# Spreading the sums of w_out over four pairs of blocks of chunk 1, and taking the last product and store in two pieces over two queues

## Chip, cores and metric

One core of one Trainium2 chip runs the whole program. The metric is device time in microseconds (us) of one execution. Lower is better. Runs of one kernel here spread over 0.3 to 5.6 us from one execution to the next, so differences below that are read from stages inside the profiles, as explained below.

## The reference

Everything is float32.

```python
# q, k, v: (8 batches, 8 heads, 576, 64)
kv = einsum('bhsd,bhse->bhde', k, v)
o = einsum('bhsd,bhde->bhse', q, kv)
rms = sqrt(mean(o * o, axis=-1) + 1e-6)
x = (o / rms * g_norm)                     # -> (4608, 512)
gate = 1 / (1 + exp(-(x @ w_gate)))        # w_gate, w_val: (512, 1536)
out = (gate * (x @ w_val)) @ w_out         # w_out: (1536, 512)
```

## The kernel before

The 4608 rows are worked in chunks of 512 (`G`). Chunk 0 is computed plainly. From chunk 1 on both layers use a seven-product scheme for 2x2 blocked matrices, so seven block products do the work of eight, at the price of sums of the operands. The sums of `x` and of the hidden activations are made for each chunk. The sums of `w_out` (`t2w`) are made once, in chunk 1, since chunk 0 still reads the plain `w_out`.

The first layer of a chunk runs six pairs of blocks. A pair issues p1, p6, p2, p7, p5, p4, p3, each for two blocks. After each of these seven comes one `slot()`, in which one small step of other work is put into the engines' streams: a step of the attention for the next chunk, or, in chunk 1, a sum of `w_out`. VectorE (DVE) reads the products out of PSUM, the memory that TensorE writes, and TensorE (PE) can begin a later product only when the bank that it writes has been read.

```python
def slot():
    if fill:
        fill.popleft()()

# first layer, one pair
one, two = block(f), block(f + NF2)
for i, (p, r) in enumerate(zip(one[0], two[0])):
    p()
    r()
    slot()
    # ... at i == 4 and 5: GpSimd makes the sums of w_gate, w_val for the next pair
one[1]()          # h * gate, VectorE, 128x512, both inputs in SBUF
two[1]()
h_sums(c, f)      # four sums on VectorE, 128x256

# the second layer, end of one group of rows
product(pc, lambda f: s12[c, f][:, t1], t2w[1], True)
tt(out=o2[:, d2], in0=pc, in1=o2[:, d2], op=ALU.add)
product(pb, lambda f: gv[c, f + NF2][:, t2], t2w[4], False)
tt(out=o2[:, d1], in0=pb, in1=o2[:, d1], op=ALU.add)
store(c, 2 + g, o2)
product(pc, lambda f: s4[c, f][:, t1], b[2, 2], False)
tt(out=o1[:, d2], in0=pc, in1=o1[:, d2], op=ALU.add)
store(c, g, o1)   # 256 KB, all issued on SyncE's queue

# the eight half sums of w_out, ahead of the attention steps in the same queue
def t2w_sum(i, in0, in1):
    for fs in (slice(0, NF2 // 2), slice(NF2 // 2, NF2)):
        fill.append(lambda fs=fs: tt(out=t2w[i][:, fs], in0=in0[:, fs], in1=in1[:, fs], op=ALU.subtract))
t2w_sum(3, b22, b12)
t2w_sum(1, b12, b11)      # written over b12
t2w_sum(2, b22, t2w[1])
t2w_sum(4, b21, t2w[2])
for c in range(1, NG):
    if c + 1 < B:
        feed(c + 1, at_ps)        # appends the steps of attention
    first_layer_fast(c)
    sums_of(c + 1)
    second_layer_fast(c)
    flush()
```

Of the kernel before, what the change touches and what calls it, by code (L numbers as in the profile page):

```python
# [14 lines left out]
ALU = mybir.AluOpType  # L15
# [4 lines left out]
def kernel(  # L20
# [11 lines left out]
    nc = tc.nc  # L32

    B, H, S, HD = q.shape
    T, DM = out.shape
# [3 lines left out]
    NJ = 6  # L39
# [13 lines left out]
    NG = T // G  # L53
# [237 lines left out]
    fill = deque()  # L291
# [5 lines that stand above are left out]
    def feed(b, at_ps):  # L297

        for n in range(NHP * b, NHP * b + NHP, 2):
            both = []  # L300

            def tile_of(i, both=both):
                def ps(kind):
                    if kind != "kv":
                        return at_ps(kind)
                    if not both:
                        both.append(at_ps(kind))
                    return both[0][:, :, HD * i:HD * i + HD]
                return ps

            one, two_ = (attention(n + i, tile_of(i)) for i in range(2))

            def kv_of_both(one=one, two_=two_):
                one[0]()
                two_[0]()

            fill.extend([kv_of_both, one[1], two_[1]])
            for steps in (one, two_):

                fill.extend(steps[2:-2] + [lambda: None] * 2 + steps[-2:])  # L320
# [7 lines left out]
    def gv_tile(c, f):  # L328
        gv[c, f] = hp.tile([P, G], FP32, tag="gv", name="gv")
        return gv[c, f]  # L330

    def sg_tile():
        return sb.tile([P, G], FP32, tag="sg", name="sg", bufs=4)

    def store(c, t, ot):

        r0 = 0
        while r0 < P:
            b, s = divmod(G * c + P * t + r0, S)
            j, p = divmod(s, NP)  # L340
            n = min(P - r0, NP - p)
            dst = out[S * b:S * b + S, :].rearrange("(p j) d -> j p d", j=NJ)[j, p:p + n, :]
            nc.sync.dma_start(out=dst, in_=ot[r0:r0 + n])
            r0 += n


    psum_at = ctx.enter_context(tc.tile_pool(name="psum_at", bufs=1, space=bass.MemoryType.PSUM))
# [3 lines left out]
    def at_ps(kind):  # L351
        return psum_at.tile([P, 2, 512], FP32, tag="at", name="at")
# [15 lines left out]
    def mm_ps():  # L368
        return psum.tile([P, 512], FP32, tag="mm", name="mm", bufs=6)
# [21 lines left out]
    def plain(c, f, ps):  # L391

        blk = Plain(c, f, ps)
        for at in range(2 * NMT):
            blk.mm(*divmod(at, NMT))
            if at in (0, 2) and late:
# [8 lines left out]
    steps = {"KV": KV, "KVO": KV_OUT, "Q": Q, "QO": Q_OUT, "U": U, "SQ": U_SQUARE, "SUM": U_SUM, "ROOT": U_ROOT,  # L405
             "NORM": U_NORM, "X": X, "XO": X_OUT}
# [16 lines left out]
    for token in order.split():  # L423
        name = token.rstrip("0123456789.")
        n = [int(i) for i in token[len(name):].split(".")]
        f = n[0]
        if name == "b":
            if f not in blks:
# [4 lines left out]
                else:  # L433
                    t = at_ps(None) if f else two0
# [57 lines left out]
    DH = DM // 2  # L492
    h1, h2 = slice(0, GH), slice(GH, G)
    tt = nc.vector.tensor_tensor
    sx, tw, s12, s4 = {}, {}, {}, {}

    def quarters(c):
        return {(i, j): xT[c][:, NK * (j - 1):NK * j, GH * (i - 1):GH * i] for i in (1, 2) for j in (1, 2)}
# [18 lines left out]
    def first_layer_fast(c):  # L517
        s, a = sx[c], quarters(c)

        def block(f):  # L520

            d = {}
            pa, pb, pc = (mm_ps()[:, h1] for _ in range(3))
            bg, bv = w["wg", f], w["wv", f]

            def product(ps, wt, xs, new):
                for m in range(NK):
                    nc.tensor.matmul(ps, wt[:, m, :], xs[:, m, :], start=(new and m == 0), stop=(m == NK - 1),  # L528
                                     skip_group_check=True)


            def p1():
                product(pa, bg[:, 0:NK], a[1, 1], True)
                d["sg"] = sg_tile()
                nc.scalar.copy(out=d["sg"][:, h2], in_=pa)  # L535

            def p6():
                product(pb, tw[f, 2], s[:, 1], True)
                d["h"] = gv_tile(c, f)
                tt(out=d["h"][:, h1], in0=pb, in1=d["sg"][:, h2], op=ALU.add)  # L540

            def p2():
                product(pa, bg[:, NK:], a[1, 2], False)
                nc.scalar.activation(out=d["sg"][:, h1], in_=pa, func=AF.Sigmoid)  # L544

            def p7():
                product(pb, tw[f, 3], a[2, 1], False)
                tt(out=d["h"][:, h2], in0=pb, in1=d["sg"][:, h2], op=ALU.add)  # L548

            def p5():  # L550
                product(pc, tw[f, 1], s[:, 0], True)
                tt(out=d["h"][:, h2], in0=pc, in1=d["h"][:, h2], op=ALU.add)

            def p4():
                product(pb, tw[f, 4], a[2, 2], False)
                tt(out=d["sg"][:, h2], in0=pb, in1=d["sg"][:, h2], op=ALU.add)  # L556
                nc.scalar.activation(out=d["sg"][:, h2], in_=d["sg"][:, h2], func=AF.Sigmoid)  # L557

            def p3():
                product(pc, bv[:, NK:], s[:, 2], False)  # L560
                tt(out=d["h"][:, h1], in0=pc, in1=d["h"][:, h1], op=ALU.add)  # L561

            def end():
                tt(out=d["h"], in0=d["h"], in1=d["sg"], op=ALU.mult)  # L564

            return [p1, p6, p2, p7, p5, p4, p3], end

        for f in range(NF2):
# [6 lines that stand above are left out]
                if f + 1 < NF2 or c + 1 < NG:  # L575
                    n = (f + 1) % NF2
                    if i == 4:
                        for k_ in (1, 2, 3):
                            w_sum(n, k_)
                            w_sum(n + NF2, k_)  # L580
                    elif i == 5:
                        w_sum(n, 4)
                        w_sum(n + NF2, 4)
            one[1]()
            two[1]()
            h_sums(c, f)
# [12 lines left out]
    def second_layer_fast(c):  # L599
        b = {(j, n): w2[:, NF2 * (j - 1):NF2 * j, DH * (n - 1):DH * n] for j in (1, 2) for n in (1, 2)}  # L600
        d1, d2 = slice(0, DH), slice(DH, DM)
        for g in range(2):
            t1, t2 = slice(P * g, P * g + P), slice(GH + P * g, GH + P * g + P)
            pa, pb, pc = (mm_ps()[:, 0:DH] for _ in range(3))

            def product(ps, hs, ws, new):
                for f in range(NF2):
                    nc.tensor.matmul(ps, hs(f), ws[:, f, :], start=(new and f == 0), stop=(f == NF2 - 1),  # L608
                                     skip_group_check=True)
                    if f % 3 == 2:  # L610
                        slot()

            product(pa, lambda f: gv[c, f][:, t1], b[1, 1], True)
            o2 = sg_tile()
            nc.scalar.copy(out=o2[:, d1], in_=pa)
            product(pb, lambda f: s12[c, f][:, t2], t2w[2], True)
            o1 = sg_tile()
            tt(out=o1[:, d2], in0=pb, in1=o2[:, d1], op=ALU.add)
            product(pa, lambda f: gv[c, f + NF2][:, t1], b[2, 1], False)
            nc.scalar.copy(out=o1[:, d1], in_=pa)  # L620
            product(pb, lambda f: gv[c, f][:, t2], t2w[3], False)
            tt(out=o2[:, d2], in0=pb, in1=o2[:, d1], op=ALU.add)
            product(pc, lambda f: s12[c, f][:, t1], t2w[1], True)
            tt(out=o2[:, d2], in0=pc, in1=o2[:, d2], op=ALU.add)
            product(pb, lambda f: gv[c, f + NF2][:, t2], t2w[4], False)
            tt(out=o2[:, d1], in0=pb, in1=o2[:, d1], op=ALU.add)
            store(c, 2 + g, o2)
            product(pc, lambda f: s4[c, f][:, t1], b[2, 2], False)
            tt(out=o1[:, d2], in0=pc, in1=o1[:, d2], op=ALU.add)
            store(c, g, o1)  # L630

    def sums_of(c):
        if c < NG:
            fill.append(lambda: fill.extendleft(reversed(x_sums(c))))
# [6 lines left out]
    for t in range(G // P):  # L641
# [3 lines left out]
        ot = sg_tile()  # L645
# [5 lines left out]
    t2w = {i: sums.tile([P, NF2, DH], FP32, name=f"t2w{i}", bufs=1) for i in (2, 3, 4)}  # L651
    t2w[1] = b12

    def t2w_sum(i, in0, in1):
        for fs in (slice(0, NF2 // 2), slice(NF2 // 2, NF2)):
            fill.append(lambda fs=fs: tt(out=t2w[i][:, fs], in0=in0[:, fs], in1=in1[:, fs], op=ALU.subtract))  # L656

    t2w_sum(3, b22, b12)
    t2w_sum(1, b12, b11)
# [4 lines left out]
    for c in range(1, NG):  # L664
        if c + 1 < B:
            feed(c + 1, at_ps)
        first_layer_fast(c)
        sums_of(c + 1)
        second_layer_fast(c)
        flush()  # L670
# [30 lines left out]
```

## Time and profile before

The median is 1112.08 us in the three runs first given, and 1112.33 us over six runs (1112.03 to 1114.88) with those made beside the changed kernel.

To compare kernels closely I cut each profile's span at two marks that the chain of waits shows: the first product of chunk 1, and the first product of chunk 2. That gives three stages.

| stage of the kernel before | us | what lies in it |
|---|---|---|
| front, to chunk 1's first product | 161.02 | loads, first attention, chunk 0 |
| chunk 1 | 123.55 | the sums of w_out, wherever they are put |
| rest, from chunk 2's first product to the end of the span | 825.49 | chunks 2 to 8, the last store |

The mark that ends chunk 1 is this line of the kernel before's chain of waits (start in us, length in us, what ran):

```profile
284.57 1.73 PE mm L528 x8
```

(The rest is taken from the view by windows, which gives a stretch to 0.01 us; the page prints the span to 0.1 only.) The other views of the kernel before are in the prediction.

### The profile page before, as it was taken

Reading aid. Unit: us, or ns where it says so; the run is one execution under the profiler, and the core shown is the slowest. Engines: PE = TensorE matmul, PEld = TensorE weight load, DVE = VectorE, ACT = ScalarE, POOL = GpSimd, SP = SyncE. Lnnn points to the kernel's source line nnn. Section 1 sums busy time; section 2 is a strip of 40 time slices with the busy share of each in tenths; the row PEclk is TensorE's granted clock in tenths of the full one; section 3 lists DMA queues with packets and bytes.
Section 4 is the critical chain, followed back from the end, with each engine's and each line's share of the span. In section 5 each row is a group of like instructions: output and inputs, shape, how many; then the busy total and the mean of one; then the engine's idle time right before and its main releaser. Section 6 shows DMA issues by size and latency. Waiting matters only on the chain.

```text
span 1110.1 us, 15195 instructions
## 1 busy us (share of the span) xinstructions
PE 1099.9 (99%) x5806; PEld 914.9 (82%) x5806; DVE 571.4 (51%) x1157; ACT 319.2 (29%) x615; POOL 279.3 (25%) x390
## 2 busy tenths in 40 slices
PE   8999999999999999999999999999999999999998
PEld 7644458888888888888888888888888888888887
DVE  4887758652355415552456336541555256615541
ACT  4754421421243213340333124321333021101110
POOL 0000025440244204330344024420444044404410
PEclk9999999999999999999999999999999999999999
DMA  9954312021201020201211020202000000010001
GB/s 248 270 173 155 146 39 54 12 54 31 73 12 54 21 73 21 54 12 29 64 46 30 19 73 12 54 16 77 22 11 1 26 13 1 1 31 8 1 1 39
DMA packets 71596, 57.61 MB, mean 52 GB/s; under 512 B 40804, under 2 KB 65380, under 8 KB 71524
## 3 DMA queue, kind: packets, MB, share of 16 engines
q1 hardware_dynamic: 71360, 56.64, 19.1%
q8 instruction: 47, 0.77, 0.3%
q14 instruction: 29, 0.21, 0.1%
q10 hardware_dynamic: 160, 0.00, 0.0%
HBM read 47.19 MB, written 9.44 MB: 51 GB/s over the span
## 4 chain that ended last, share of the span: by engine, by line
PE 96%; DVE 2%; issue 1%; DMA 0%; ACT 0%; SPq 0%; DVEq 0%; ACTq 0%
PE mm L528 51%; PE mm L608 26%; PE mm L379 6%; PE mm L471 4%; PE at L250 2%; PE at L379 2%; PE at L221 2%; PE at L235 1%; PE at L276 1%; PE two L250 1%; DMA q<-in_q_dram 0%; DVE gv L564 0%; PE two L221 0%; PE two L235 0%; DVE t2w L656 0%
## 5 line engine op out<-in xcount | busy, mean ns | idle before, releaser
L514 POOL TENSOR_TENSOR tw<-gv 128x256 f32<-128x256 f32 x192 | 140.0, 740 | 779.9 <-PE mm L528 628.1
L528 PE MATMUL mm<-xT,tw 128*128 128x256 f32 x768 | 182.4, 380 | 1.0 <-DVE gv L540 1.0
L528 PE MATMUL mm<-sx,tw 128*128 128x256 f32 x768 | 182.4, 380 | 0.0
L528 PE MATMUL mm<-xT,gv 128*128 128x256 f32 x768 | 181.6, 379 | 0.0
L528 PEld LDWEIGHTS mm<-xT,gv 128*128 128x128 f32 x768 | 145.5, 190 | 20.1 <-issue 0.5
L528 PEld LDWEIGHTS mm<-xT,tw 128*128 128x128 f32 x768 | 143.3, 190 | 20.3 <-issue 1.8
L528 PEld LDWEIGHTS mm<-sx,tw 128*128 128x128 f32 x768 | 144.1, 190 | 19.0
L514 POOL TENSOR_TENSOR tw<-gv,tw 128x256 f32<-128x256 f32 x192 | 144.4, 773 | 0.0
L557 ACT ACTIVATE sg<-sg 128x256 f32<-128x256 f32 x96 | 39.9, 417 | 213.1 <-DVE sg L556 213.1
L548 DVE TENSOR_TENSOR gv<-mm,sg 128x256 f32<-128x256 f32 x96 | 40.8, 425 | 99.8 <-PE mm L528 99.8
L528 PE MATMUL mm<-sx,gv 128*128 128x256 f32 x384 | 90.9, 379 | 0.0
L608 PE MATMUL mm<-t2w,gv 128*128 128x256 f32 x384 | 89.0, 379 | 0.0
L608 PE MATMUL mm<-w,gv 128*128 128x256 f32 x384 | 88.3, 379 | 0.0
L608 PE MATMUL mm<-w,s 128*128 128x256 f32 x384 | 88.1, 379 | 0.0
L608 PEld LDWEIGHTS mm<-w,s 128*128 128x128 f32 x384 | 72.9, 190 | 9.9
L608 PEld LDWEIGHTS mm<-t2w,gv 128*128 128x128 f32 x384 | 72.5, 190 | 9.6
L608 PEld LDWEIGHTS mm<-w,gv 128*128 128x128 f32 x384 | 72.4, 190 | 9.6
L535 ACT COPY sg<-mm 128x256 f32<-128x256 f32 x96 | 35.8, 373 | 154.4 <-PE mm L528 154.4
L528 PEld LDWEIGHTS mm<-sx,gv 128*128 128x128 f32 x384 | 72.1, 190 | 9.4
L564 DVE TENSOR_TENSOR gv<-gv,sg 128x512 f32<-128x512 f32 x96 | 78.7, 860 | 0.2
L561 DVE TENSOR_TENSOR gv<-mm,gv 128x256 f32<-128x256 f32 x96 | 40.7, 424 | 47.9 <-PE mm L528 47.5
L544 ACT ACTIVATE sg<-mm 128x256 f32<-128x256 f32 x96 | 36.3, 384 | 100.5 <-PE mm L528 100.5
(96 smaller groups left out, 1137.0 us busy)
## 6 DMA issues: line engine op xcount, KB each, us to landing
k<-in_k_dram SPq DMA_DIRECT2D x32, 288.0 KB, 4.6
v<-in_v_dram SPq DMA_DIRECT2D x32, 288.0 KB, 4.8
q<-in_q_dram SPq DMA_DIRECT2D x64, 144.0 KB, 3.1
st<-in_moe_w_gate_dram SPq DMA_DIRECT2D x12, 512.0 KB, 5.4
st<-in_moe_w_val_dram SPq DMA_DIRECT2D x12, 512.0 KB, 6.9
st<-in_moe_w_out_dram SPq DMA_DIRECT2D x12, 512.0 KB, 4.1
out_dram<-sg SPq DMA_DIRECT2D x24, 192.0 KB, 2.3
out_dram<-sg SPq DMA_DIRECT2D x24, 128.0 KB, 2.4
```

What stands on the lines that cost most here:

```text
L250: nc.tensor.matmul(d["u"][:, i], qT[:, M * i:M * i + MU], kvs[n % 2], start=True, stop=True)
L379: nc.tensor.matmul(self.ps[i], w[("wg", "wv")[i], self.f][:, m, :], xT[self.c][:, m, :], start=(m == 0), stop=(m == NMT - 1), skip_group_c ...
L471: nc.tensor.matmul(ps[t], gv[0, f][:, P * t:P * t + P], w["wo", f], start=(f == 0), stop=(f == NFT - 1), skip_group_check=True)
L514: nc.gpsimd.tensor_tensor(out=tw[f, i], in0=b[in0], in1=b[in1] if isinstance(in1, tuple) else tw[f, in1], op=ALU.subtract)
L528: nc.tensor.matmul(ps, wt[:, m, :], xs[:, m, :], start=(new and m == 0), stop=(m == NK - 1), skip_group_check=True)
L535: nc.scalar.copy(out=d["sg"][:, h2], in_=pa)
L544: nc.scalar.activation(out=d["sg"][:, h1], in_=pa, func=AF.Sigmoid)
L548: tt(out=d["h"][:, h2], in0=pb, in1=d["sg"][:, h2], op=ALU.add)
L557: nc.scalar.activation(out=d["sg"][:, h2], in_=d["sg"][:, h2], func=AF.Sigmoid)
L561: tt(out=d["h"][:, h1], in0=pc, in1=d["h"][:, h1], op=ALU.add)
L564: tt(out=d["h"], in0=d["h"], in1=d["sg"], op=ALU.mult)
L608: nc.tensor.matmul(ps, hs(f), ws[:, f, :], start=(new and f == 0), stop=(f == NF2 - 1), skip_group_check=True)
```

## The change

The intent is, first, that VectorE should never have a row of sums of w_out ahead of the adds that free PE's banks: the eight sums are put into slots 3 and 4 of each of the first four pairs, two per pair. Second, that the program should end sooner after the last arithmetic: the left half of the last rows is stored as soon as it is done, the last two products on the right half are cut into two halves of 128 columns, and the stores of the last pieces alternate over two queues.

```diff
-    def store(c, t, ot):
+    def store(c, t, ot, cols=slice(0, DM), queues=(nc.sync,)):
 ...
-            nc.sync.dma_start(out=dst, in_=ot[r0:r0 + n])
+            queues[i % len(queues)].dma_start(out=dst, in_=ot[r0:r0 + n, cols])
 ...
+            last = (c, g) == (NG - 1, 1)
+            parts = [slice(0, DH // 2), slice(DH // 2, DH)] if last else [slice(0, DH)]
+            pcs = [mm_ps()[:, 0:x.stop - x.start] for x in parts]
 ...
+            if last:
+                store(c, g, o1, d1)
 ...
-            product(pc, lambda f: s12[c, f][:, t1], t2w[1], True)
-            tt(out=o2[:, d2], in0=pc, in1=o2[:, d2], op=ALU.add)
+            for pc, x in zip(pcs, parts):
+                product(pc, lambda f: s12[c, f][:, t1], t2w[1][:, :, x], True)
+                o2x = o2[:, DH + x.start:DH + x.stop]
+                tt(out=o2x, in0=pc, in1=o2x, op=ALU.add)
 ...
-            product(pc, lambda f: s4[c, f][:, t1], b[2, 2], False)
-            tt(out=o1[:, d2], in0=pc, in1=o1[:, d2], op=ALU.add)
-            store(c, g, o1)
+            for pc, x in zip(pcs, parts):
+                product(pc, lambda f: s4[c, f][:, t1], b[2, 2][:, :, x], False)
+                y = slice(DH + x.start, DH + x.stop)
+                tt(out=o1[:, y], in0=pc, in1=o1[:, y], op=ALU.add)
+                if last:
+                    store(c, g, o1, y, (nc.sync, nc.scalar))
+            if not last:
+                store(c, g, o1)
 ...
+    w2_sums = deque()
 ...
-            fill.append(lambda fs=fs: tt(out=t2w[i][:, fs], ...))
+            w2_sums.append(lambda fs=fs: tt(out=t2w[i][:, fs], ...))
 ...
+        if c == 1:
+            steps = list(fill)
+            fill.clear()
+            while w2_sums or steps:
+                fill.append(w2_sums.popleft() if w2_sums and len(fill) % 7 in (3, 4) else steps.pop(0))
         first_layer_fast(c)
```

The change adds one line above the first layer's code, so line 528 of the kernel before is line 529 after, and so on (540 is 541, 564 is 565); the second layer's product, 608, is 613.

More of the change, by code (lines that the diff above doesn't have):

```diff
@@ L333, in sg_tile @@
         return sb.tile([P, G], FP32, tag="sg", name="sg", bufs=4)
-    def store(c, t, ot):
-        r0 = 0
+    def store(c, t, ot, cols=slice(0, DM), queues=(nc.sync,)):
+        r0 = i = 0
         while r0 < P:
@@ L341, in store @@
             n = min(P - r0, NP - p)
-            dst = out[S * b:S * b + S, :].rearrange("(p j) d -> j p d", j=NJ)[j, p:p + n, :]
-            nc.sync.dma_start(out=dst, in_=ot[r0:r0 + n])
+            dst = out[S * b:S * b + S, :].rearrange("(p j) d -> j p d", j=NJ)[j, p:p + n, cols]
+            queues[i % len(queues)].dma_start(out=dst, in_=ot[r0:r0 + n, cols])
             r0 += n
+            i += 1
     psum_at = ctx.enter_context(tc.tile_pool(name="psum_at", bufs=1, space=bass.MemoryType.PSUM))
@@ L603, in second_layer_fast @@
             t1, t2 = slice(P * g, P * g + P), slice(GH + P * g, GH + P * g + P)
-            pa, pb, pc = (mm_ps()[:, 0:DH] for _ in range(3))
+            pa, pb = (mm_ps()[:, 0:DH] for _ in range(2))
+            last = (c, g) == (NG - 1, 1)
+            parts = [slice(0, DH // 2), slice(DH // 2, DH)] if last else [slice(0, DH)]
+            pcs = [mm_ps()[:, 0:x.stop - x.start] for x in parts]
             def product(ps, hs, ws, new):
@@ L652 @@
     t2w[1] = b12
+    w2_sums = deque()
     def t2w_sum(i, in0, in1):
         for fs in (slice(0, NF2 // 2), slice(NF2 // 2, NF2)):
-            fill.append(lambda fs=fs: tt(out=t2w[i][:, fs], in0=in0[:, fs], in1=in1[:, fs], op=ALU.subtract))
+            w2_sums.append(lambda fs=fs: tt(out=t2w[i][:, fs], in0=in0[:, fs], in1=in1[:, fs], op=ALU.subtract))
     t2w_sum(3, b22, b12)
```

## The prediction

> **What bounds the kernel now.** I read the page first: engine shares, then the chain that ended last.
>
> ```profile
> PE 1099.9 (99%) x5806; PEld 914.9 (82%) x5806; DVE 571.4 (51%) x1157; ACT 319.2 (29%) x615; POOL 279.3 (25%) x390
> PE 96%; DVE 2%; issue 1%; DMA 0%; ACT 0%; SPq 0%; DVEq 0%; ACTq 0%
> ```
>
> TensorE (PE) is 99% busy and 96% of the chain, at full clock. Nothing here removes a matmul, so only PE's own waits and the end of the program can change. Next, the waits of PE in 161 to 246 us, the first layer of chunk 1 (the stretch the first half of the change touches); the same view for 284 to 366 us, chunk 2, lists none.
>
> ```profile
> PE mm L528 <- DVE gv L540: 1.0, 2, 0.7
> PE at L235 <- DVE kv L227: 0.8, 1, 0.8
> ```
>
> The chain for the same stretch shows where:
>
> ```profile
> 161.02 8.65 PE mm L528 x40
> ...
> 175.44 2.36 DVE gv L564 x2
> ...
> 179.38 0.87 DVE t2w L656
> 180.25 0.35 DVE gv L540
> 180.60 0.14 issue
> 180.74 3.69 PE mm L528 x16
> ...
> 220.79 0.43 DVE gv L540
> ```
>
> At 180.74 PE waits for VectorE (DVE), which is late because eight sums of w_out (L656) stand ahead of its other work; by then the last of them is in the way. At 220.8 it waits for the same kind of add (L540), after a head's normalization, with no w_out sum near. At 235 it waits for the two copies of a head's kv. The timeline says what a sum of w_out costs: 0.95 us alone, 1.31 to 1.50 us where GpSimd (POOL) runs beside it, as here:
>
> ```profile
> 165.79 0.95 DVE L656 TENSOR_TENSOR w<-w 128x768 f32<-128x768 f32 x1
> ...
> 171.93 1.50 DVE L656 TENSOR_TENSOR t2w<-w 128x768 f32<-128x768 f32 x1
> 172.58 2.13 POOL L514 TENSOR_TENSOR tw<-gv 128x256 f32<-128x256 f32 x2
> ```
>
> Last, the end, in the timeline:
>
> ```profile
> 1103.45 2.75 PE L608 MATMUL mm<-w,s 128*128 128x256 f32 x12
> 1103.65 0.42 DVE L626 TENSOR_TENSOR sg<-mm,sg 128x256 f32<-128x256 f32 x1 [2.17 <-PE mm L608]
> 1104.10 3.41 SPq L343 DMA_DIRECT2D out_dram<-sg  x4
> 1106.24 0.42 DVE L629 TENSOR_TENSOR sg<-mm,sg 128x256 f32<-128x256 f32 x1 [2.17 <-PE mm L608]
> ```
>
> The last add ends at 1106.66, the last of four store issues on one queue at 1107.51, the span at 1110.1: 3.4 us after the last arithmetic.
>
> **What the Trainium skill says.** "TensorE: Matmul & The Clock Gate", section LDWEIGHTS: a weight load costs its columns over 1.2, 107 ns for 128. The trace agrees when spacing is read instead of duration: ten warm-up loads of 128x128 take 1.20 us, that is (1.20 - 0.19) / 9 = 0.112 us apart, though each is drawn 0.19 long. "SBUF — State Buffer", section Who interferes with whom: a VectorE instruction with two SBUF inputs contends with a GpSimd instruction that reads SBUF; the 0.95 against 1.31 to 1.50 us agrees. "DMA: Bandwidth & Descriptors", section Issuing engines are not separate DMA queues: issuing on several engines saves only the issue time. No run yet shows a store on the second queue. Same page, Anatomy of one DMA: about 2.0 us of a transfer is fixed; the stores here land in 1.6 to 3.7 us, median 2.3, the last two about 2.2 and 2.0.
>
> **The change, part 1: the sums of w_out.** Before, seven sums fill the slots of the first pair of blocks and one the second's; the first of them is free, as it runs at 150.75, before chunk 1 starts. After, the order on VectorE is: no sum ahead of chunk 1; two in each of the first four pairs, after the two adds of p7 and after the two adds of p5. The steps of attention start eight slots earlier and meet the old order again at slot 26. PE's work is the same, only its order differs. So I wrote out the order of each engine for both kernels and added durations: a product of one block 4 x 0.216 = 0.86 us (seven products of two blocks 12.1), adds from PSUM 0.42, L564 0.66 alone and 1.04 beside GpSimd, the four sums of h 0.36 apart, reduce 0.81, reciprocal 0.23, normalization 0.83, sums of w_out 0.95 first and 1.49 second (the second falls where GpSimd has begun), table load 1.28, root 0.30, sigmoid 0.43, x copies 1.05, and 0.2 from PE's end to a reader. For the kernel before this gives waits of 0.69 at 179.9, 0.57 at 220.7, 0.99 at 233.9, with small ones 2.81 in all, and the second layer at 245.11 (trace: 245.32). So the sheet is good to some 0.2 us here. For the changed kernel it says:
> - First pair: VectorE ends its sums of h at 179.3, and the add that frees the bank at 179.8, while PE, with the kv and u matmuls now inside, asks for it at 181.5. The 0.69 is gone.
> - Second pair: second sum of w_out until 187.1, both adds of p4 until 188.0, sigmoid 188.4, table load and root 190.1, reciprocal and normalization 191.3, two L564 192.6, sums of h 194.0, add of the next p6 194.45. PE wants the bank at 194.07: a new wait of 0.48 with latency.
> - Third pair: second sum until 200.2, adds of p4 201.0, sigmoid 201.5, the x copies behind it on ScalarE (ACT) until 202.5. The transposes of q, in the slot after, need the bank that these copies read; PE is there at 201.46: a new wait of 1.26. The order of the changed kernel lists that wait on ScalarE.
> - Fourth pair: two sums now precede the normalization: the wait of 0.57 grows to 0.80. The one of 0.99 stays.
>
> Sum 3.93 against 2.81: 1.1 us slower. With 1.30 for the contended sum it is 246.03 against 245.11, 0.9 slower; with 0.95, even. I take +0.8.
>
> **Part 2: the last product and store.** The last group's s12 and s4 products each become two halves of 128 columns: 24 matmuls at the weight load's 0.112 = 2.69 us in place of 12 x 0.216 = 2.59, +0.1 each, +0.2 on the path. The last add covers 128 columns: 256 cost 0.425 and 1 ns per further column (0.69 for 512), so 0.29: -0.13. The store of the left half goes out some 10 us earlier, the first quarter 1.3 us earlier; what is left is 64 KB in place of 256 KB, on two queues. The second issue (1107.1 to 1107.5) no longer stands behind the first: -0.4. The data of the last store move from 1107.55 to 1108.6; a quarter of them, in rows of 512 bytes, perhaps 0.4 in place of 1.0, partly the same saving as the issue: -0.4 more. Sum -0.75. No WAR wait appears in the order: the last adds wait for PE alone.
>
> Total: 1112.08 + 0.8 - 0.75 = 1112.1 us.
>
> **The rivals.**
> - The spread does what it intends: the wait at 180.74 goes and none comes. For it: half of VectorE's time is free on average, and chunk 2 runs with no wait. Against it: VectorE's slack in a pair with a head's work (12.1 + 1.1 of PE against some 9.5) is about as long as two sums. It would give -1.0 here and, with the tail, 1110.3.
> - Weight loads bind the halves: if each really took its drawn 0.19 us, 48 x 0.19 = 9.1 us in place of 5.2, +3.9 and 1115.5. Against it: the spacing of 0.112, and ten matmuls of L250 with 128 columns and new weights in 1.09 us.
> - The second queue is slow to start: its only transfers before (g_col, at the program's start) took 0.58 us to issue and 3.6 us to land, in tiny pieces. If the last piece lands so, the tail loses its gain and up to 1 us more: 1113.5. Against it: those were 4-byte rows at a busy start.
>
> **Range and chances.** Part 1 may be -1.0 to +1.5, part 2 -1.3 to +0.2; together some 1.2 each way eight times in ten: 1110.8 to 1113.1. 2% is 22 us, far beyond every rival, so within 2% has 0.99.
>
> **What would show it.** In the waits of PE in 161 to 246 us: the one of 0.7 at 180 gone, a wait of about 1.3 of the transposes of q (L235) on ScalarE's x copies near 201, one of about 0.5 near 194, one of about 0.8 on L541 near 221; the second layer starting near 246. If it starts before 245, part 1 is wrong. At the end: 24 matmuls of a halved product in 2.7 us, the last add near 0.29, and the span ending about 2.7 us after it in place of 3.4. A halved product of 4 us, or more than 3 us after the last add, would make part 2 wrong.

## The result, and the profile after

The changed kernel took 1112.55 us (median of six runs, 1111.58 to 1112.95), the kernel before 1112.33. Ratios here are the mean time of one kernel's fast runs over that of the other's of the same rounds, so not quite the ratio of the medians. It is 0.9997, with a 95% interval of 0.9984 to 1.001. A second set of five runs (below) gave 0.9993. The output was correct. By the times alone the change does nothing that can be told from zero.

The stages say more:

| | front | chunk 1 | rest |
|---|---|---|---|
| before | 161.02 | 123.55 | 825.49 |
| after | 162.69 | 123.68 | 824.80 |

Chunk 1 is 0.13 us longer, the rest is 0.69 us shorter, and the front of this one profile is 1.67 us longer. The front explains why the span of the profile went up, from 1110.1 to 1111.2, although the two changed stages together lost 0.56 us. The front holds nothing of the change but one sum of w_out less, ahead of chunk 1; its granted clock was lower in this profile ("Open", below).

The page of the changed kernel, engine shares (busy us, share of the span, instructions; PEld is TensorE loading weights, POOL is GpSimd):

```profile
PE 1101.6 (99%) x5830; PEld 920.2 (83%) x5830; DVE 571.6 (51%) x1159; ACT 318.7 (29%) x615; POOL 280.8 (25%) x390
```

The reader is to see 24 more matmuls and two more VectorE instructions, the cut products and adds, and the same VectorE time: the sums were moved, not removed.

The waits of PE in 155 to 290 us of the changed kernel (what waited, for what, total us, times, longest):

```profile
PE mm L529 <- DVE gv L541: 0.9, 1, 0.9
PE at L235 <- DVE kv L227: 0.8, 1, 0.8
PE at L235 <- ACT xT L285: 0.3, 1, 0.3
```

Of the two old waits on the add L541 (L540 before) one is gone; the other has grown to 0.9 us. The wait on the copies of kv has stayed. The last line is new: the transposes of q wait for ScalarE's (ACT's) copies of x. The chain of waits over the same stretch says where each is:

```profile
162.69 1.73 PE mm L529 x8
...
179.87 15.54 PE mm L529 x72
195.41 0.50 PE at L276 x5
195.91 3.50 PE mm L529 x16
...
199.85 1.23 DVE t2w L672
201.08 0.34 DVE sg L557
...
201.45 0.75 ACT sg L558 x2
202.20 0.94 ACT xT L285 x3
...
203.18 0.71 PE at L235 x6
...
218.47 1.22 DVE gv L565
...
219.71 0.84 DVE s L595
...
222.58 0.43 DVE gv L541
...
223.14 1.97 PE mm L529 x8
...
247.28 5.18 PE mm L613 x24
```

From 179.87 to 195.41 PE runs 72 matmuls with no gap, over the place where it used to wait at 180.74. At 199.85 the second sum of the third pair is on the chain: it holds up the adds of p4 (L557), these the sigmoid (L558), and the x copies (L285) stand behind the sigmoid on ScalarE. PE starts the transposes at 203.18. At 218.47 the multiplications by the gate (L565), the sums of h, and, behind them, the normalization (L267) stand ahead of the add that frees PE's bank.

The timeline of the third pair (start, length, engine, line, operation, output<-input, shapes, count, and in brackets the idle time before and what ended it):

```profile
199.77 1.31 DVE L672 TENSOR_TENSOR t2w<-w 128x768 f32<-128x768 f32 x1
200.23 2.13 POOL L515 TENSOR_TENSOR tw<-gv,tw 128x256 f32<-128x256 f32 x2
...
201.00 0.74 DVE L557 TENSOR_TENSOR sg<-mm,sg 128x256 f32<-128x256 f32 x2
...
203.18 0.71 PE L235 MATMUL at<-ident,q 96*128 96x96 f32 x6 [0.34 <-ACT xT L285]
```

Two things to see. The sum beside GpSimd took 1.31 us, not 1.5, and the next instruction started 1.23 us after it did. And two adds from PSUM took 0.74 us together, though each is 0.42 us long: the second starts 0.34 us after the first.

The end of the program, in the timeline of the changed kernel:

```profile
1100.07 2.84 PE L613 MATMUL mm<-w,s 128*128 128x128 f32 x24
...
1105.33 2.84 PE L613 MATMUL mm<-w,s 128*128 128x128 f32 x24
...
1106.87 0.29 DVE L640 TENSOR_TENSOR sg<-mm,sg 128x128 f32<-128x128 f32 x1 [0.91 <-PE mm L613]
...
1108.21 0.29 DVE L640 TENSOR_TENSOR sg<-mm,sg 128x128 f32<-128x128 f32 x1 [1.05 <-PE mm L613]
```

The last add ends at 1108.50 and the span at 1111.2, 2.7 us later, against 3.4 us before. The store issues of the last pieces, in the DMA view (output<-input, queue, count, KB, us from issue to landing), first of the kernel before, 1106 to 1110 us, then of the changed kernel, 1107.9 to 1110 us:

```profile
out_dram<-sg SPq DMA_DIRECT2D x1, 192.0 KB, 2.2
out_dram<-sg SPq DMA_DIRECT2D x1, 64.0 KB, 2.0
```

```profile
out_dram<-sg SPq DMA_DIRECT2D x1, 48.0 KB, 1.5
out_dram<-sg ACTq DMA_DIRECT2D x1, 16.0 KB, 1.7
```

The final pieces are a quarter in size, go out at the same time on two queues, and land in 1.5 and 1.7 us.

### The profile page after: what moved, and what is told of

It is laid out like the page before. It is cut to its first block, busy times and chain, and to the rows that moved or that the text cites. A ratio compares the mean times of both kernels' runs of the same rounds, so it can differ in the third digit from the quotient of the medians.

```text
span 1111.2 us, 15257 instructions
## 1 busy us (share of the span) xinstructions
PE 1101.6 (99%) x5830; PEld 920.2 (83%) x5830; DVE 571.6 (51%) x1159; ACT 318.7 (29%) x615; POOL 280.8 (25%) x390
## 4 chain that ended last, share of the span: by engine, by line
PE 96%; DVE 1%; SPq 1%; DMA 1%; ACT 0%; issue 0%; DVEq 0%
PE mm L529 51%; PE mm L613 26%; PE mm L380 6%; PE mm L472 4%; PE at L250 2%; PE at L380 2%; PE at L221 2%; PE at L235 1%; PE at L276 1%; DMA q<-in_q_dram 1%; PE two L250 1%; PE two L221 0%; PE two L235 0%; PE two L276 0%; SPq L79 0%; SPq L88 0%
## 5 line engine op out<-in xcount | busy, mean ns | idle before, releaser
L515 POOL TENSOR_TENSOR tw<-gv,tw 128x256 f32<-128x256 f32 x192 | 146.8, 785 | 0.0
L558 ACT ACTIVATE sg<-sg 128x256 f32<-128x256 f32 x96 | 39.7, 417 | 217.3 <-DVE sg L557 217.3
L613 PE MATMUL mm<-w,s 128*128 128x256 f32 (+1 forms) x408 | 88.3, 367 | 0.0
L565 DVE TENSOR_TENSOR gv<-gv,sg 128x512 f32<-128x512 f32 x96 | 78.6, 858 | 0.2
```

The costliest lines, as they stand in the source:

```text
L515: nc.gpsimd.tensor_tensor(out=tw[f, i], in0=b[in0], in1=b[in1] if isinstance(in1, tuple) else tw[f, in1], op=ALU.subtract)
L558: nc.scalar.activation(out=d["sg"][:, h2], in_=d["sg"][:, h2], func=AF.Sigmoid)
L565: tt(out=d["h"], in0=d["h"], in1=d["sg"], op=ALU.mult)
L613: nc.tensor.matmul(ps, hs(f), ws[:, f, :], start=(new and f == 0), stop=(f == NF2 - 1), skip_group_check=True)
```

## The experiments

All twelve kernels gave correct results. "Chunk 1" and "rest" are the stages of the table above, from each kernel's profile. Ratios are to the kernel before on the same chip. The runs came from two sessions; in the second the kernel before itself went from 1112.2 to 1114.8 us while the session lasted, so its medians (1114.48 us over 11 runs, 1113.77 over 12) are no good yardstick, and the stages decide. One slip stands in the texts: where they give 123.8 us for chunk 1 of the changed kernel, 123.68 is right.

| kernel | median us | ratio, 95% interval | front | chunk 1 | rest |
|---|---|---|---|---|---|
| after_again | 1112.16 | 0.9993 (0.998 to 1.0005) | 162.04 | 123.67 | 824.82 |
| only_sums | 1112.91 | 1.0001 (0.9988 to 1.0015) | 161.39 | 123.66 | 825.49 |
| only_tail | 1111.8 | 0.9991 (0.9979 to 1.0004) | 161.33 | 123.55 | 824.82 |
| early_sums | 1110.59 | 0.9981 (0.9967 to 0.9995) | 165.29 | 120.81 | 825.50 |
| tail_one_queue | 1113.24 | 0.9992 (0.9978 to 1.0005) | 161.54 | 123.55 | 825.02 |
| tail_no_split | 1112.79 | 0.9993 (0.9978 to 1.0008) | 162.27 | 123.56 | 824.93 |
| early_both | 1109.15 | 0.9966 (0.995 to 0.9983) | 161.46 | 120.82 | 824.80 |
| sums_gap | 1111.97 | 0.9982 (0.9967 to 0.9996) | 161.57 | 123.21 | 825.50 |
| slots_kept | 1113.63 | one run | 161.64 | 124.73 | 825.48 |
| no_fourth_pair | 1114.64 | one run | 162.47 | 124.90 | 825.48 |
| no_third_pair | 1112.27 | one run | 161.48 | 123.52 | 825.49 |
| slots_kept_2 | 1112.7 | 0.9995 (0.9978 to 1.0012) | 161.78 | 122.99 | 825.48 |

### The two parts apart, and the change again

Edits: after_again is the changed kernel unaltered. only_sums is the kernel before with the sums' part of the diff alone; only_tail is the kernel before with the tail's part alone:

```diff
 # only_tail, against the changed kernel
-            w2_sums.append(lambda fs=fs: tt(...))
+            fill.append(lambda fs=fs: tt(...))
 ...
-        if c == 1:
-            ... (the interleaving)
```

> The changed kernel unaltered, as a control beside the others. The two parts add: 0.26 - 0.70 = -0.4 us against before. If the front (first loads) decides the scatter, its chunk 1 (123.8) and its remainder (824.8) repeat to 0.1 us while the start of chunk 1 varies by 1 us or more.

> Part 1 alone, end as before. Theory A (part 1 only moves PE's waits about): chunk 1, from its first product to chunk 2's, takes 123.8 us as in the changed kernel (123.55 before); the rest, from chunk 2's first product to the span's end, 825.5 as before; the time is 0.2 to 0.3 us above the kernel before, within its scatter. Theory B (the spread removes PE's waits, and the gain was hidden by a slow start of the first loads in the changed kernel's profiled run): chunk 1 near 121 us, 2 to 3 us below before.

> Part 2 alone, sums as before. Theory A: chunk 1 at 123.55 us; from chunk 2's first product to the end 824.8 (825.5 before); time 0.7 us below before. Theory B (the halved product eats what the smaller last store saves): 825.5, time equal to before.

The parts add up: only_sums changes chunk 1 by 123.66 - 123.55 = +0.11 us and leaves the rest within its scatter; only_tail leaves chunk 1 as it was and changes the rest by 824.82 - 825.49 = -0.67. after_again repeats both stages of the changed kernel to 0.02 us. The timed runs of none of the three can be told from the kernel before. So part 1 costs 0.1 us and not 0.8, and part 2 gains 0.7.

### The tail taken apart

```diff
 # tail_one_queue: only_tail, with
-                    store(c, g, o1, y, (nc.sync, nc.scalar))
+                    store(c, g, o1, y, (nc.sync,))
 # tail_no_split: only_tail, with
-            parts = [slice(0, DH // 2), slice(DH // 2, DH)] if last else [slice(0, DH)]
+            parts = [slice(0, DH)]
```

> Part 2 alone (sums as before), but the last two pieces both on the first queue. From chunk 2's first product to the span's end: 824.8 with two queues, 825.5 before. Theory A (the second issue of 0.4 us behind the first is worth its length): 825.2. Theory B (the last data and their landing decide, the issue lies beside them): 824.8.

> Part 2 alone without halves: the left half of the columns stored early, the right half (256 columns) in one product, one add and one store over two queues. Theory A (what counts is fewer bytes after the last add and one issue less; the halves trade 0.2 us of PE for 0.13 us of the add and 64 KB less to move): 824.8 to 825.0. Theory B (the halving is what earns the gain): 825.4 or more.

Without the second queue the rest is 825.02 us, so the second queue is worth 825.02 - 824.82 = 0.20 us, half of what the prediction gave it and midway between the two theories. Without the cut the rest is 824.93, so cutting the products is worth 0.11 us net of its two times 0.07 us on PE. What is left, 825.49 - 824.93 = 0.56 us, comes from storing the left half early and so having 128 KB in place of 256 KB at the end, over two queues. Each of these small differences rests on one profile, with stages that repeat to 0.02 us in the profiles of like tails.

### The sums out of the first layer

If the sums cost nothing where they are put, chunk 1 should be as short with them as without. Four sums can be had in another order, since b22 - (b12 - b11) = (b22 - b12) + b11, and then only the sum that overwrites b12 has to wait until chunk 0 has read it:

```diff
 # early_sums on the kernel before; early_both on only_tail
-            fill.append(lambda fs=fs: tt(out=t2w[i][:, fs], ..., op=ALU.subtract))
+            tt(out=t2w[i][:, fs], in0=in0[:, fs], in1=in1[:, fs], op=op)
     t2w_sum(3, b22, b12)
-    t2w_sum(1, b12, b11)
-    t2w_sum(2, b22, t2w[1])
+    t2w_sum(2, t2w[3], b11, ALU.add)
     t2w_sum(4, b21, t2w[2])
 ...
         first_layer_fast(c)
+        if c == 1:
+            t2w_sum(1, b12, b11)
```

> Tail as before; six of the eight sums of w_out run between chunk 0 and chunk 1 (the second matrix is made from the third, so nothing that chunk 0 still reads is overwritten), where VectorE idles for 11.9 us before chunk 1's first add; the other two run after the first layer of chunk 1; attention steps start at slot 0 as in chunk 2. Theory A (PE's waits in chunk 1 are all VectorE being late through these sums or through the steps that they displaced): chunk 1 takes what chunk 2 takes, 120.8 us, 2.7 us less than before, no wait of PE on VectorE in it; time near 1109.5 against 1112.2. Theory B (the waits at 221 and 235 belong to chunk 1's attention work itself): only the wait at 180 goes, chunk 1 at 122.5, time 1 us below before.

> The early sums of w_out with the end of the changed kernel: chunk 1 120.8 us and the rest 824.8, 3.4 us less than before from chunk 1's first product on; time about 1109.0 against 1112.4.

Chunk 1 falls to 120.81 us, 2.74 less than before and as long as chunk 2 in all fourteen profiles (120.81 to 120.82), and in both kernels the view of PE's waits lists none in 155 to 290 us. The chain of early_both, at the marks:

```profile
161.46 1.73 PE mm L529 x8
...
282.28 1.73 PE mm L529 x8
```

early_both is the best kernel: 1109.15 us, ratio 0.9966 (0.995 to 0.9983), about 3.8 us under the kernel before by the ratio (0.0034 of 1112.3) and 3.4 us by its stages (2.73 and 0.69). Its interval and that of the changed kernel (0.9984 to 1.001) just fail to meet, but the interval of the changed kernel's second set (0.998 to 1.0005) does meet it, so the times alone do not settle this and the stages do. One of its six runs took 1114.44 us. In early_sums VectorE made six of the half sums from 155.0 to 162.9 us (in early_both from 151.3 to 159.2), while PE finished chunk 0, where VectorE otherwise had little to do.

### Other slots for the sums

```diff
 # sums_gap: only_sums, with
-    ... if w2_sums and len(fill) % 7 in (3, 4) else ...
+    ... if w2_sums and len(fill) % 7 in (1, 2) else ...
```

> Part 1 alone with the pairs of sums two slots earlier (after the adds of p6, where VectorE idles for about 2 us and GpSimd has not begun). Theory A (what part 1 gives back is the sums' place: contended, and ahead of the adds of p4): each pair takes 2 x 0.95, the wait of the q transposes on ScalarE's copies near 202 goes; chunk 1 between 122.5 and 123.2. Theory B (the eight sums and the displaced steps cost the same wherever they stand): 123.6.

Chunk 1 is 123.21 us, 0.45 less than in only_sums and 0.34 less than before, at the edge of what theory A allowed; the wait that it said would go did not. The waits on L540 and on the x copies fall from 0.8 and 0.3 us to 0.3 and 0.2; that on the copies of kv stays at 0.8. So an earlier slot within a pair helps, but 2.4 of the 2.85 us over early_sums remain. This asked for a cause other than where the sums stand in a pair.

### The slots without the sums

Placing a sum in a slot does two things: it loads VectorE, and it moves every later step of attention one slot on. slots_kept makes the sums as early_sums does, yet keeps the eight slots, empty. slots_kept_2 is the same with the last sum made later:

```diff
 # slots_kept: the sums as in early_sums; the interleaving of only_sums, fed with
+    for _ in range(4):
+        w2_sums.extend([lambda: None] * 2)
 # slots_kept_2: as slots_kept, but the sum over b12 inside chunk 1's second layer
             tt(out=o1[:, d2], in0=pb, in1=o2[:, d1], op=ALU.add)
+            if (c, g) == (1, 0):
+                t2w_sum(1, b12, b11, now=True)
```

> All eight sums of w_out outside the first layer of chunk 1 (as in early_sums), but their eight slots kept, empty, so that the steps of attention stand as in the changed kernel. Theory A (the sums make VectorE late): chunk 1 is 120.8 to 121.2 us as with early_sums (120.81), no wait of PE in it. Theory B (it is the steps of attention, displaced to those slots, that collide): near 123, with the waits at the transposes of q and after the fourth pair.

> slots_kept again, with the two sums that run after the first layer moved behind the second product of the second layer, since in slots_kept they stood ahead of a head's normalization there and PE waited 1.8 us for it. Theory B (the displaced steps of attention make most of chunk 1's excess): chunk 1 at 122.9 to 123.0 us, with waits of some 0.2 at the q transposes near 202, 0.5 near 221 and 1.0 near 235. Theory A (the sums make it): 120.8 to 121.2.

slots_kept read 124.73 us, but 1.8 us of that is a wait of its own making: the transposes of x (L276) wait for a normalization (L267) that stands behind my postponed sum on VectorE. slots_kept_2 is the clean version. Its waits of PE in 155 to 290 us:

```profile
PE at L235 <- DVE kv L227: 0.8, 1, 0.8
PE mm L528 <- DVE gv L540: 0.3, 1, 0.3
PE at L235 <- ACT xT L285: 0.2, 1, 0.2
```

These three are the waits of the kernels with sums, with no sum of w_out in the first layer at all. They add up to 1.3 us only, because the view counts from the modelled end of the matmul before. From the start of one matmul to the start of the next, PE loses 0.34 us at the x copies, 0.58 after the fourth pair, 0.98 at the copies of kv, and 0.17 at a normalization in the second layer, each beyond the usual 0.216 us: 2.07 us in all, nearly the whole excess over early_sums. Chunk 1 is 122.99 us. Of the 123.66 - 120.81 = 2.85 us by which only_sums exceeds early_sums, 122.99 - 120.81 = 2.18 us come from the moved steps of attention alone, and 123.66 - 122.99 = 0.67 us from the sums' own time on VectorE. The theory that VectorE is late because of the sums falls as the main cause. What takes its place is shown as to the size and read from the chain as to the way: with eight slots in front of them, or among them, the attention steps fall on other places in a pair than in chunk 2, which lists no wait. A normalization and the copies of kv then come to stand at the border between two pairs, behind the gate's multiplications and the sums of h and close to the add that PE waits for (the chain above shows the order at 218 to 223 us).

### One pair without its sums

```diff
 # no_fourth_pair: only_sums, the fourth pair's slots empty, its sums after the first layer
-    t2w_sum(4, b21, t2w[2])
+    w2_sums.extend([lambda: None] * 2)
 # no_third_pair: only_sums, the third pair's slots empty, its sums before chunk 1, as
+    t2w_sum(2, b22, b12, now=True); t2w_sum(2, t2w[2], b11, ALU.add, now=True)
```

> Part 1 alone (123.66), the two sums in the fourth pair of blocks replaced by empty slots and run after the first layer. Theory A: the wait of 1.0 us after the fourth pair falls to the 0.5 of before or to nothing, the one of the transposes of q stays at 0.5: chunk 1 at 122.7 to 123.2. Theory B (that wait comes from the head's normalization alone): 123.6.

> Part 1 alone, the two sums in the third pair replaced by empty slots and made between chunk 0 and chunk 1. Theory A: the wait of the transposes of q on ScalarE's copies goes (its chain runs through the second sum of the third pair): chunk 1 0.5 us shorter, 123.2, the wait after the fourth pair unchanged at 1.0. Theory B (the copies are late whatever VectorE does): 123.6.

The waits of no_fourth_pair, 155 to 290 us:

```profile
PE at L276 <- DVE sq L267: 1.7, 1, 1.7
PE at L235 <- DVE kv L227: 0.8, 1, 0.8
PE mm L528 <- DVE gv L540: 0.3, 1, 0.3
PE at L235 <- ACT xT L285: 0.3, 1, 0.3
```

The first line is again made by my postponed sums; without it chunk 1 would be about 124.90 - 1.7 = 123.2 us. The third line answers the question: taking the fourth pair's sums away brings the wait after that pair from 0.8 us (only_sums) to 0.3, so the sums do lengthen this wait, and a remainder is there without them. no_third_pair brings the wait for the x copies only from 0.3 to 0.2 us and chunk 1 from 123.66 to 123.52: those copies come late even with no sum in their pair, while the wait after the fourth pair reads 0.9 us against 0.8. The two runs agree with the division by slots_kept_2, small for the sums, large for the moved steps.

## Why the prediction was right or wrong

**The total.** It said 1112.1 us, and the medians were 1112.55 and, in the second set, 1112.16. But its two terms, +0.8 and -0.75, were to cancel, and the measured ones are +0.1 and -0.7. The step that failed is the first term: the new waits of part 1 were booked too large. From the stages the changed kernel should be 0.6 us faster than the one before. The ratios (0.9997 and 0.9993, that is -0.3 and -0.8 us) allow this but do not show it: the spread of the front is larger. The agreement of the total is partly luck.

**Part 1, the wait at 180.** Right: it is gone, 72 matmuls run over the place.

**Part 1, the new wait of 0.48 near 194.** Wrong: PE goes from the transposes at 195.41 to the next product at 195.91 with no wait. VectorE was on time. An error that would make it so, though no run isolates it, is in a term used throughout the ledger: adds from PSUM that stand one after the other were booked at 0.42 us each, and start 0.34 apart (0.74 for two).

**Part 1, the new wait of 1.26 at the transposes of q.** Right in place and in releaser, ScalarE's x copies; too large. It is 0.3 us by the profile (0.49 by the starts of the matmuls before and after it, in only_sums). The mis-sized terms are the second sum, booked at 1.49 us and costing 1.23 to the next start, and again the adds. Shifted by the later start of chunk 1 in this run (162.69 against 161.02), the ledger had the adds of p4 done at 202.7; they were done at 201.74, about 1.0 us sooner, which covers the whole miss (1.26 against 0.49 or 0.3).

**Part 1, the waits after the fourth pair and at 233.9.** The first grew as the ledger said, and by more: from 0.3 us by the profile to 0.9. The ledger booked the four sums of h 0.36 us apart, but the first of them took 0.83 us here, twice its 0.42. GpSimd worked beside it. The second stayed, as it said.

**Part 1, the sum.** By the starts of the matmuls, in the kernel before and in only_sums, the changes are -0.94 at 180, +0.49 at the transposes of q, and +0.50 after the fourth pair (from 0.58 to 1.08), which is +0.05 us. The stage grew by 0.11 us there and by 0.13 in the changed kernel. The ledger had -0.69, +0.48 near 194 (which never came), +1.26 and +0.23. The mechanism, one wait exchanged for others, held; the sizes did not. The prediction's own test, "if it starts before 245, part 1 is wrong", did not catch this: the front had moved that absolute time, and even with the front taken off the second layer began at 245.4, inside the test. Its first matmul starts at 247.12, which is 84.43 us after chunk 1's start, against 245.32 - 161.02 = 84.30 in the kernel before: +0.13. The ledger had 246.03 against 245.11: +0.92. A test on this difference would have shown the miss.

**Part 2.** -0.75 was foreseen, -0.69 was found. By terms: the halves cost 2.67 us from start to start (1100.07 to the next product at 1102.74) in place of 2.59, so +0.15 for two, where +0.2 was said; the last add took 0.29 us, as said; the second queue gave 0.2 and not 0.4; the smaller last transfer therefore gave more than its 0.4, by subtraction about 0.5. The prediction had warned that the two overlap. So two terms missed in opposite directions and the sum came out, which is partly luck too.

**The rivals.** That the spread frees PE outright (-1.0) is refuted by the stage and by the waits. The prediction's argument against it was weak by its own numbers: a slack of 12.1 + 1.1 - 9.5 = 3.7 us is not "about as long" as two sums of 0.95 and 1.49. That the weight loads take 0.19 us each (+3.9) is refuted: a halved product took 2.67 us, not 4. (By the prediction's own terms this rival came to 1112.1 + 3.9 - 0.2 = 1115.8, not 1115.5.) That the second queue is slow to start is refuted: 16 KB on it landed in 1.7 to 1.8 us, and the 3.6 us of g_col at the program's start was no guide.

**What it did not see.** The ledger looked for waits caused by VectorE's load. The larger cost of having the sums in slots, in the changed kernel, is the 2.2 us from attention steps pushed off their places. For the kernel before, with its sums in the first eight slots, no run with empty slots was made; its waits at 221 and 235 (0.34 and 0.81 us) have the sizes of those in slots_kept_2, so the same is likely, not shown. The waits that the prediction read at 220.8 "with no w_out sum near" and at 235 were the hint: they were already there, of a kind that chunk 2 does not have.

**Open.** Why the front varies by up to 4 us is not settled, but the record narrows it. In the three profiles with the longest fronts (early_sums 165.29, the changed kernel 162.69, no_fourth_pair 162.47) the granted clock of TensorE was below 1.00 in 20 to 40 us: 0.83, 0.94 and 0.94. In the other eleven it stayed at 1.00 there, and their fronts are 161.02 to 162.27. In the view by windows (window, length, busy us and instructions of PE, PEld, DVE, ACT and POOL, then clock, DMA share, GB/s), early_sums and then the kernel before:

```profile
20.00:40.00 20.00, 19.66 (x156) 14.25 (x155) 13.70 (x22) 10.25 (x20) 0.00 (x0) 0.83 1.04 241
```

```profile
20.00:40.00 20.00, 19.95 (x193) 14.26 (x192) 16.26 (x29) 12.02 (x24) 0.00 (x0) 1.00 1.16 268
```

A clock of 0.83 over 20 us is worth 3.4 us by estimate, most of the 4.27 us by which that front is longer than that of the kernel before. So the longer span of the changed kernel's profile goes with the clock and not with the change: after_again kept its clock at 1.00, with a front of 162.04. What lowers the clock is not shown. Slow loads of q, which stand early in most of the chains, are no sufficient cause: in only_sums the chain waits 7.97 us for one, and its front is 161.39. Whole runs mostly agree: the four runs of early_both at clock 1.0 took 1108.85 to 1109.22 us, the one at 0.997 took 1114.44; but one run of the kernel before took 1114.73 at 1.0.

## What to carry to other kernels

When work is put into numbered slots between other steps, count what the slot moves as well as what the work costs: here empty slots alone made 2.2 of the 2.85 us. Before spreading a one-time cost over a busy stretch, look for a stretch where its engine is idle anyway, even if the algebra has to be reordered to get there; that was worth 2.7 us, the spread nothing. And when a change is smaller than the scatter of the runs, cut the span at marks that both kernels have: stages repeated to 0.02 us in profiles whose fronts differed by 4.

## What the Trainium skill lacked or had wrong

- "SBUF — State Buffer", section Who interferes with whom: it says that VectorE with two inputs in SBUF contends with GpSimd's reads, and gives no size for it. Here, where the two ran side by side, a sum of w_out went from 0.95 us to 1.31 to 1.50, a sum of h from 0.42 to 0.83, and a pair of GpSimd's sums from 1.4 to 2.1 us.
- "DMA: Bandwidth & Descriptors", section Anatomy of one DMA: its fixed part of about 2.0 us is given for DMAs that GpSimd issues, so it is no yardstick for these stores, which SyncE and ScalarE issue; the section has no such figure for their queues. Here 48 KB landed 1.5 us after issue and 16 KB in 1.7.
- Same page, section Issuing engines are not separate DMA queues: right that a second queue saves only issue time; what it saved here was less, 0.20 us where one issue takes about 0.4.
- "TensorE: Matmul & The Clock Gate", section LDWEIGHTS: its 107 ns for 128 columns fits the spacing here (24 matmuls of 128 columns with new weights in 2.67 us, 0.111 each), but no run shows that the load sets it: half of the 0.216 us of a matmul of 256 columns would be 0.108 as well. The trace draws each load about 0.19 us long; the section doesn't warn of that.
